# Reordering three weight and gate loads and six matmuls in the first microseconds of a gated attention/MLP kernel

## The chip, the cores and the metric

The kernel runs on one core of a Trainium2 chip. The metric is the device time of one execution in microseconds (us). The kernel before the change takes 206.35 us, the median of 4 runs (206.03 to 206.88).

## What is computed

One input `x` of 2048 rows by 512 goes through two branches, and a gate of one number per row mixes them:

```python
g = sigmoid((x * gate_w).sum(-1, keepdims=True))
# branch a: linear attention, 32 heads of 16, softmax feature maps of q and k
# branch b: gated MLP that mixes along the sequence
z  = gelu(x @ w_in)                    # 2048 x 1376
z1 = z[..., :688]
z2 = layernorm(z[..., 688:])
b  = (z1 * (w_sp @ z2 + b_sp)) @ w_out
out = g * a + (1 - g) * b
```

Only the very first part of branch b matters here: `x @ w_in[:, 688:]` for the first two tiles of 128 rows of `x`, and the dot product of these rows with `gate_w`.

## The kernel before, in words

The 2048 rows are 16 tiles of 128. For a matmul a tile of `x` must lie transposed in SBUF (`xT`), with the 512 inputs as four blocks `dt` of 128 partitions. Tiles 2 to 15 are transposed by DMA on the way in. Tiles 0 and 1 are loaded straight (`xs`, lines 119 and 120) and transposed by TensorE with an identity matrix (`x_T`, line 278).

The right half of `w_in` is held in `w_z2`, also in four blocks `dt`, each 128 partitions by 688 columns (172 KB), and each fetched by a DMA of its own (`load_z2w`, line 116). A tile's `z2` is a sum over the four blocks, in two halves `j` of 344 columns that lie in two PSUM banks: eight matmuls. The gate rides along: the four blocks of `gate_w`, loaded as four rows into `gaterow` (line 124), are turned by one small matmul (`gate_T`, line 288) and put as column 688 into `w_z2`, so that the second half is 345 columns wide and its last column is the gate's dot product.

`z2_first_two` (line 215) does this for tiles 0 and 1 together, in an order written out by hand, since the weights are still arriving. It begins with seven matmuls on constants into a buffer that is overwritten later (`warm_up`), then the transposes, then:

- `one(tt, dt, j)` is one of the matmuls of tile `tt`, block `dt`, half `j`.
- `z_part(tt, 0, 344, True)` is block 0's second half without the gate's column, since that column isn't there yet. `z_part(tt, 344, 345, False)` adds the missing column later.
- `gate_T()` may stand anywhere ahead of the first matmul that is 345 wide.

TensorE (PE) and ScalarE (ACT) run their instructions in the order of the program text; nothing rearranges them. DMAs are issued by SyncE (SP) and ScalarE, each with a queue of its own (in the profile, q1 is SP's queue and q10 is ScalarE's). Before the change the order of issue is

- SP: `x` tile 0, block 0, block 2, block 3, then the transposing loads of tiles 2 and 3, the left half of `w_in` (line 135), and all else that is loaded;
- ScalarE: `x` tile 1, block 1, gate row, then a table load and a small activation (line 127) that prepare the first gelu.

After `z2_first_two` come `z2` of tiles 2 and 3, `z1` of tiles 0 to 3, and so on for all tiles. The second, longer part of the kernel does the attention branch and the mixing along the sequence. Its matmuls are the largest groups of the profile, and the change touches none of them.

Of the kernel before, what the change touches and what calls it, by code (L numbers as in the profile page):

```python
# [14 lines left out]
P = 128  # L15
# [6 lines left out]
HF = FH // 2  # L22
NT = S // P
NDT = D // P
# [11 lines left out]
def kernel(  # L36
# [14 lines left out]
    nc = tc.nc  # L51
# [41 lines left out]
    gaterow = early.tile([P, P], BF16, name="gaterow")  # L93
# [11 lines left out]
        out=ramp[:, 0, :], data0=ones32[:, :], data1=zeros[:, :], initial=0.0,  # L105
# [4 lines left out]
    for q in range(4):  # L110
        qs = slice(32 * q, 32 * q + 32)
        nc.vector.tensor_tensor(
            out=ident[qs, qs], in0=ramp[qs, 0, :], in1=ramp[qs, 1, :], op=ALU.is_equal)
    nc.gpsimd.memset(brow[:], 0.0)
    nc.gpsimd.memset(wphi[:], 0.0)
    def load_z2w(eng, dt):
        eng.dma_start(out=w_z2[:, dt, 0:FH], in_=w_in_v[:, dt, FH:F])

    nc.sync.dma_start(out=xs[:, 0, :], in_=x2[0:P, :])  # L119
    nc.scalar.dma_start(out=xs[:, 1, :], in_=x2[P:2 * P, :])  # L120
    load_z2w(nc.sync, 0)
    load_z2w(nc.scalar, 1)
    load_z2w(nc.sync, 2)
    nc.scalar.dma_start(out=gaterow[0:NDT, :], in_=gate_w.rearrange("(dt p) -> dt p", p=P))
    load_z2w(nc.sync, 3)
    scrap = early.tile([P, 1], BF16, name="scrap")
    nc.scalar.activation(
        out=scrap[:, :], in_=nc.const_aps.tensor(1.0, [P, 1], BF16), func=AF.Gelu_apprx_tanh)
# [5 lines left out]
    for h in range(2):  # L134
        nc.sync.dma_start(
            out=w_z1[:, 2 * h:2 * h + 2, :], in_=w_in_v[:, 2 * h:2 * h + 2, 0:FH])
    for i in range(4, 8):
        x_dma_T(i)
    for q in range(2, NCH):
        nc.sync.dma_start_transpose(  # L140
            out=xT[:, :, q * CH:(q + 1) * CH], in_=x2[q * CH:(q + 1) * CH, :]
        )
    nc.sync.dma_start(out=brow[0:NT, :], in_=B_b_sp.rearrange("(t p) -> t p", p=P))
    for qk in (1, 0):
        nc.sync.dma_start_transpose(
            out=wqkT[:, qk * NDT:(qk + 1) * NDT, :], in_=A_wqkv[:, qk * D:(qk + 1) * D])
# [4 lines left out]
    for h in range(2):  # L151
        nc.sync.dma_start(
            out=wv_sb[:, 2 * h:2 * h + 2, :],
            in_=A_wqkv[h * 2 * P:(h + 1) * 2 * P, 2 * D:3 * D].rearrange("(dt p) n -> p dt n", p=P),
        )
    for q in range(NCH):
        nc.sync.dma_start_transpose(
            out=wspT[:, :, q * CH:(q + 1) * CH], in_=B_w_sp[q * CH:(q + 1) * CH, :]
# [4 lines left out]
        out=mask4[:], in_=mask4[:], pattern=[[-32, NG]],  # L163
# [3 lines left out]
        out=mask4[:], in_=mask4[:], pattern=[[32, NG]],  # L167
# [3 lines left out]
        out=mask64[:, :, :], in_=mask4[:, :, None].to_broadcast([P, NG, DH]))  # L171
# [7 lines left out]
    def next_turn(kind, n):  # L179
        turn[kind] += 1  # L180
        return f"{kind}{(turn[kind] - 1) % n}"

    def zp_tile():
        return psA.tile([P, 2, CH], FP32, name="zp", tag=next_turn("zp", 3))

    def pq_tile(shape, dtype=FP32):
        return psF.tile(shape, dtype, name="pq", tag=next_turn("pq", 2))

    def z_one(zp, tt, wt, w, dt, j, skip=False):
        n = HF if j == 0 else w - HF  # L190
        nc.tensor.matmul(  # L191
            zp[:, j, 0:n], lhsT=xT[:, dt, tt * P:(tt + 1) * P],
            rhs=wt[:, dt, j * HF:j * HF + n],
            start=(dt == 0), stop=(dt == NDT - 1), skip_group_check=skip,
        )
# [8 lines left out]
    def z2_out(tt, zp):  # L204
        z2v = z2all[:, tt, :].rearrange("p (j n) -> p j n", j=2)
        nc.scalar.activation(out=z2v, in_=zp[:, :, 0:HF], func=AF.Gelu_apprx_tanh)  # L206
        nc.vector.tensor_copy(out=glog[:, tt:tt + 1], in_=zp[:, 1, HF:HF + 1])
        for j in range(2):
            nc.vector.bn_stats(out=bn6[:, tt, j, :], in_=z2v[:, j, :])  # L209
        nc.vector.bn_aggr(out=mv[:, tt, :], in_=bn6[:, tt, :, :].rearrange("p j s -> p (j s)"))  # L210
# [4 lines left out]
    def z2_first_two():  # L215
        zps = [zp_tile() for _ in range(2)]
        tp1 = psA.tile([P, 2, P], BF16, name="tp1", tag=next_turn("zp", 3))
        turn["zp"] -= 1

        def warm_up(n, w=CH):  # L220
            for _ in range(n):
                nc.tensor.matmul(
                    zps[0][:, 1, 0:w], lhsT=nc.const_aps.tensor(1.0, [P, P], BF16),
                    rhs=nc.const_aps.tensor(1.0, [P, w], BF16), start=True, stop=True)

        def one(tt, dt, j):
            z_one(zps[tt], tt, w_z2, FH + 1, dt, j, skip=True)

        def z_part(tt, c0, c1, start):
            nc.tensor.matmul(  # L230
                zps[tt][:, 1, c0:c1], lhsT=xT[:, 0, tt * P:(tt + 1) * P],
                rhs=w_z2[:, 0, HF + c0:HF + c1], start=start, stop=False, skip_group_check=True)

        warm_up(6)
        warm_up(1, P)
        x_T(0, 0, 1, pq_tile([P, 1, P], BF16)[:, :, :])
        x_T(0, 1, NDT, pq_tile([P, 3, P], BF16)[:, :, :])
        x_T(1, 0, 2, tp1[:, :, :])
        x_T(1, 2, NDT, pq_tile([P, 2, P], BF16)[:, :, :], on_act=True)
        one(0, 0, 0)  # L240
        z_part(0, 0, HF, True)
        gate_T()
        one(0, 1, 0)
        one(1, 0, 0)
        z_part(1, 0, HF, True)
        one(1, 1, 0)
        for tt in range(2):
            one(tt, 1, 1)
        for tt in range(2):
            one(tt, 2, 0)  # L250
            one(tt, 2, 1)
            z_part(tt, HF, HF + 1, False)
        for tt in range(2):
            one(tt, 3, 0)
            one(tt, 3, 1)
            z2_out(tt, zps[tt])
# [21 lines left out]
    def x_T(i, d0, d1, tp, on_act=False):  # L278
        for dt in range(d0, d1):
            nc.tensor.transpose(tp[:, dt - d0, :], xs[:, i, dt * P:(dt + 1) * P], ident[:, :])  # L280
        dst = xT[:, d0:d1, i * P:(i + 1) * P]
        if on_act:
            nc.scalar.copy(out=dst, in_=tp)
        else:
            with tc.high_priority():
                nc.vector.tensor_copy(out=dst, in_=tp)

    def gate_T():
        gt = pq_tile([P, NDT])
        nc.tensor.matmul(gt[:, :], lhsT=gaterow[:, :], rhs=ident[:, 0:NDT], start=True, stop=True)  # L290
        nc.vector.tensor_copy(out=w_z2[:, :, FH], in_=gt[:, :])
# [27 lines left out]
    with tc.manual_schedule(engines={mybir.EngineType.PE, mybir.EngineType.Activation}):  # L319
        z2_first_two()  # L320
        z2_tile(2)
        z2_tile(3)
        for c in range(NCH):
            ts = list(range(c * 4, c * 4 + 4))
            for tt in ts:
                if c > 0:
                    z2_tile(tt)
                if c >= 2 and tt % 4 == 1:
                    later = fold(3 - c)
            for tt in ts:  # L330
                z1_tile(tt)
                if c >= 2 and tt % 2 == 0:
                    later.pop(0)()
            z2_norm(ts)
            if c == 1:
                b_T()
                turn["zp"] += 1
# [306 lines left out]
```

## Time and profile before

| | us |
|---|---|
| median of 4 runs | 206.35 |
| the profiled execution | 207.08 |
| its span (first to last instruction) | 205.3 |
| TensorE busy in the span | 201.1 (98%) |
| VectorE busy | 130.4 (63%) |
| ScalarE busy | 74.6 (36%) |
| first `z2` matmul begins | 5.07 |
| first gelu of `z2` begins (tile 0 done) | 8.00 |

Times within an execution are counted from the start of the span. PE is TensorE's matmuls, PEld its weight loads, DVE is VectorE, POOL is GpSimd. "SPq" and "ACTq" in front of an operation mean that the engine's sequencer issues a DMA; the number beside it is the time of the issue, not of the transfer. The ends of matmuls are modelled, so starts are the safer thing to read: the distance between two starts is what a matmul costs in a stream.

### The profile page before, as it was taken

What the parts mean: (1) busy time and instruction counts of PE and PEld (TensorE: products, weight loads), DVE (VectorE), ACT (ScalarE), POOL (GpSimd) and SP (SyncE); (2) the same over time, 40 slices, a digit from 0 to 9 for tenths busy, and PEclk for the clock granted to TensorE, in tenths of its full rate; (3) what the DMA queues carried; (4) which work ended last, traced back from release to release, by engine and by line L of the source; (5) the groups of instructions that cost most, each with busy time, mean ns of one, the idle gap of its engine ahead of it and who ended that gap; (6) DMA issues with size and microseconds to landing.
All of it is one profiled execution on the core that took longest, in us unless ns stands there. A gap on an engine that the chain in (4) does not pass through costs nothing.

```text
span 205.3 us, 3996 instructions
## 1 busy us (share of the span) xinstructions
PE 201.1 (98%) x1557; PEld 120.1 (59%) x1557; DVE 130.4 (63%) x283; ACT 74.6 (36%) x122; POOL 45.6 (22%) x76
## 2 busy tenths in 40 slices
PE   7999999999999999999999999999999999999994
PEld 3666666665666555556565666555555555665642
DVE  4377565746977677969797788555566645633332
ACT  3456677786222233333424032222251136002303
POOL 3020202020532326244242442222204220200000
DMA  6999499999998026940413228763566458452933
GB/s 197 255 207 189 92 243 210 249 191 267 189 251 180 3 38 148 315 84 14 91 30 63 51 38 110 142 117 74 103 165 80 90 107 188 58 96 54 155 65 104
DMA packets 89931, 27.22 MB, mean 133 GB/s; under 512 B 84184, under 2 KB 89912, under 8 KB 89912
## 3 DMA queue, kind: packets, MB, share of 16 engines
q1 hardware_dynamic: 87744, 24.99, 63.0%
q10 hardware_dynamic: 2168, 1.98, 3.6%
q8 instruction: 12, 0.20, 0.4%
q14 instruction: 7, 0.06, 0.1%
HBM read 4.15 MB, written 2.10 MB: 30 GB/s over the span
## 4 chain that ended last, share of the span: by engine, by line
PE 96%; DMA 2%; SPq 0%; DVE 0%; issue 0%
PE mm L454 36%; PE zp L191 18%; PE mm L355 14%; PE mm L515 8%; PE mm L509 7%; PE mm L395 7%; PE kvacc L411 2%; DMA w_z<-in_B_w_in_dram 2%; PE at L467 2%; PE mm L520 1%; PE zp L307 0%; PE at L478 0%; PE zp L230 0%; SPq L119 0%; PE pq L307 0%; DVE ob L527 0%
## 5 line engine op out<-in xcount | busy, mean ns | idle before, releaser
L454 PE MATMUL mm<-z2all,wspT 128*128 128x344 bf16 x512 | 79.9, 309 | 0.0
L454 PEld LDWEIGHTS <-wspT 128*128 128x128 bf16 x512 | 49.0, 98 | 25.3
L191 PE MATMUL zp<-w_z,xT 128*128 128x344 bf16 (+1 forms) x254 | 38.4, 311 | 0.6 <-DMA w_z<-in_B_w_in_dram 0.6
L359 ACT ACTIVATE eq<-mm 128x512 bf16<-128x512 f32 x32 | 17.4, 595 | 51.4 <-PE mm L355 25.7
L363 DVE TENSOR_REDUCE zs<-eq 128x64 f32<-128x1024 bf16 x16 | 19.5, 1220 | 20.1 <-ACT eq L359 20.1
L191 PEld LDWEIGHTS <-xT 128*128 128x128 bf16 x254 | 24.5, 98 | 12.0
L359 ACT ACTIVATE ek<-mm 128x512 bf16<-128x512 f32 x32 | 17.3, 601 | 27.1 <-PE mm L355 27.1
L459 DVE SCALAR_TENSOR_TENSOR ucat<-mm,bT,z1all 128x344 bf16<-128x344 f32 x32 | 17.4, 544 | 15.1 <-PE mm L454 15.1
L372 POOL TENSOR_TENSOR eq<-eq,ratio 128x512 bf16<-128x512 bf16 x16 | 16.9, 1056 | 44.6 <-DVE ratio L371 36.6
L531 ACT ACTIVATE ob<-mm,g_inv 128x512 bf16<-128x512 f32 (+1 forms) x15 | 10.1, 679 | 33.1 <-PE mm L520 28.5
L363 DVE TENSOR_REDUCE zs<-ek 128x64 f32<-128x1024 bf16 x16 | 19.2, 1208 | 2.8 <-ACT ek L359 2.8
L515 PE MATMUL mm<-wspT,uT 128*128 128x512 bf16 (+2 forms) x85 | 20.1, 367 | 0.0
L355 PEld LDWEIGHTS <-xT 128*128 128x128 bf16 x128 | 12.2, 98 | 12.0
L372 POOL TENSOR_TENSOR ek<-ek,ratio 128x512 bf16<-128x512 bf16 x16 | 16.9, 1056 | 2.2 <-DVE ratio L371 1.7
L509 PE MATMUL mm<-wspT,oT 128*128 128x512 bf16 (+2 forms) x68 | 16.6, 366 | 0.0
L355 PE MATMUL mm<-wq_p,xT 128*128 128x512 bf16 x64 | 16.4, 379 | 0.0
L395 PE MATMUL mm<-wv_sb,xT 128*128 128x512 bf16 x64 | 16.4, 379 | 0.0
L355 PE MATMUL mm<-wk_p,xT 128*128 128x512 bf16 x64 | 16.3, 379 | 0.0
L209 DVE BATCH_NORM_STATS2 bn<-z2all 128x6 f32<-128x344 bf16 x32 | 14.9, 502 | 0.0
L206 ACT ACTIVATE z2all<-zp 128x688 bf16<-128x688 f32 x16 | 11.8, 743 | 8.3 <-PE zp L191 8.2
L260 ACT ACTIVATE z1all<-zp 128x688 bf16<-128x688 f32 x16 | 11.9, 743 | 5.1 <-PE zp L191 4.7
L515 PEld LDWEIGHTS <-uT 128*128 128x128 bf16 x85 | 8.1, 98 | 9.4 <-issue 0.2
(77 smaller groups left out, 142.8 us busy)
## 6 DMA issues: line engine op xcount, KB each, us to landing
out_dram<-ob ACTq DMA_DIRECT2D x12, 128.0 KB, 2.5
wspT<-in_B_w_out_dram SPq DMA_DIRECT2D x2, 640.0 KB, 4.9
w_z<-in_B_w_in_dram SPq DMA_DIRECT2D x2, 344.0 KB, 4.6
w_z<-in_B_w_in_dram SPq DMA_DIRECT2D x3, 172.0 KB, 3.8
wv_sb<-in_A_wqkv_dram SPq DMA_DIRECT2D x2, 256.0 KB, 2.8
wspT<-in_A_wo_dram SPq DMA_DIRECT2D x2, 256.0 KB, 3.7
out_dram<-ob SPq DMA_DIRECT2D x3, 128.0 KB, 1.8
uT<-ucat SPq DMA_TRANSPOSE x16, 2.8
```

What stands on the lines that cost most here:

```text
L191: nc.tensor.matmul(zp[:, j, 0:n], lhsT=xT[:, dt, tt * P:(tt + 1) * P], rhs=wt[:, dt, j * HF:j * HF + n], start=(dt == 0), stop=(dt == NDT ...
L209: nc.vector.bn_stats(out=bn6[:, tt, j, :], in_=z2v[:, j, :])
L260: nc.scalar.activation(out=z1all[:, tt, :].rearrange("p (j n) -> p j n", j=2), in_=zp[:, :, 0:HF], func=AF.Gelu_apprx_tanh,)
L355: nc.tensor.matmul(ps[:, :], lhsT=xT[:, dt, tt * P:(tt + 1) * P], rhs=w[:, dt, :], start=(dt == 0), stop=(dt == NDT - 1))
L359: nc.scalar.activation(out=e[:, :, a, :], in_=ps[:, :].rearrange("p (h f) -> p h f", f=DH), func=AF.Exp, scale=1.0 - 2.0 * a)
L363: nc.vector.tensor_reduce(out=z[:].rearrange("p h a -> p (h a)"), in_=e[:].rearrange("p h a f -> p (h a) f"), axis=AX.X, op=ALU.add,)
L372: nc.gpsimd.tensor_tensor(out=e[:, :, 1, :], in0=e[:, :, 1, :], in1=ratio[:, :, None].to_broadcast([P, H, DH]), op=ALU.mult)
L395: nc.tensor.matmul(v_ps[:, :], lhsT=xT[:, dt, tt * P:(tt + 1) * P], rhs=wv_sb[:, dt, :], start=(dt == 0), stop=(dt == NDT - 1))
L454: nc.tensor.matmul(gp[:, 0:HF], lhsT=wspT[:, st, tt * P:(tt + 1) * P], rhs=z2all[:, st, j * HF:(j + 1) * HF], start=(st == 0), stop=(st == ...
L459: nc.vector.scalar_tensor_tensor(out=ucat[tt % NU][:, c0 + j * HF:c0 + (j + 1) * HF], in0=gp[:, 0:HF], scalar=bT[:, tt:tt + 1], in1=z1all[ ...
L509: nc.tensor.matmul(acc, lhsT=oTs[tt][:, g, :], rhs=wo_t[:, g, c0:c1], start=start and g == 0, stop=stop and g == NG - 1)
L515: nc.tensor.matmul(acc, lhsT=uTs[tt][:, i + ft, :], rhs=w_main[i][:, ft, c0:c1], start=start and ft == 0, stop=False)
```

## The change

Two orders change, and nothing else. On ScalarE the gate row is issued second and block 1 third, instead of the other way round. SP's DMAs keep their order. On TensorE the matmuls that need only block 0 come first for both tiles, with `gate_T` between the second tile's two, and block 1 is used afterwards.

```diff
     nc.sync.dma_start(out=xs[:, 0, :], in_=x2[0:P, :])
     nc.scalar.dma_start(out=xs[:, 1, :], in_=x2[P:2 * P, :])
     load_z2w(nc.sync, 0)
+    nc.scalar.dma_start(out=gaterow[0:NDT, :], in_=gate_w.rearrange("(dt p) -> dt p", p=P))
+    load_z2w(nc.sync, 2)
     load_z2w(nc.scalar, 1)
-    load_z2w(nc.sync, 2)
-    nc.scalar.dma_start(out=gaterow[0:NDT, :], in_=gate_w.rearrange("(dt p) -> dt p", p=P))
     load_z2w(nc.sync, 3)
...
         one(0, 0, 0)
         z_part(0, 0, HF, True)
+        one(1, 0, 0)
         gate_T()
+        z_part(1, 0, HF, True)
         one(0, 1, 0)
-        one(1, 0, 0)
-        z_part(1, 0, HF, True)
         one(1, 1, 0)
```

The order on TensorE, block by block, is then: before `0 0 | gate | 1 0 0 1`, after `0 0 0 | gate | 0 1 1` (the digits are the blocks `dt` that the matmuls of 344 columns read). From there on both kernels do the same: the second halves of block 1, then blocks 2 and 3.

Each DMA counts its landing on one of eight semaphores, given out in turn. With the swap the gate row takes the one that block 1 had, and block 1 the gate row's. SP's later issue of tile 4's transposing load (line 131) waits for the semaphore that block 1 had before, and so for the gate row after; that of tile 6 waits for block 1 instead of the gate row.

## The prediction

> **What bounds the kernel now.** I read the page first, its busy times and the chain that ended last:
>
> ```profile
> PE 201.1 (98%) x1557; PEld 120.1 (59%) x1557; DVE 130.4 (63%) x283; ACT 74.6 (36%) x122; POOL 45.6 (22%) x76
> ...
> PE 96%; DMA 2%; SPq 0%; DVE 0%; issue 0%
> ```
>
> TensorE is the bound, and 2% of the chain is a DMA. The list of what PE waited for says which:
>
> ```profile
> PE zp L222 <- PEq L628: 0.8, 1, 0.8
> PE zp L191 <- DMA w_z<-in_B_w_in_dram: 0.6, 1, 0.6
> ```
>
> These two are all of it. The same list for 8 us to the end is empty: once past the first two tiles PE waits for no other engine and no DMA. So whatever the start gains or loses by about 8 us is handed to the end one for one, and nothing else in the kernel can pay or charge. The chain of the first 9 us shows how the start hangs together:
>
> ```profile
> 1.25 3.78 DMA w_z<-in_B_w_in_dram
> 5.03 0.04 issue
> 5.07 0.45 PE zp L191
> ```
>
> Block 0 is issued at 1.25, has landed at 5.03, and the first z2 matmul starts at 5.07. The timeline shows what stands around it:
>
> ```profile
> 1.24 0.46 ACTq L117 DMA_DIRECT2D w_z<-in_B_w_in_dram  x1
> ...
> 1.74 0.57 ACTq L124 DMA_DIRECT2D gaterow<-in_gate_w_dram  x1
> ...
> 4.21 0.15 PEld L191 LDWEIGHTS <-xT 128*128 128x128 bf16 x1
> ...
> 5.07 0.45 PE L191 MATMUL zp<-w_z,xT 128*128 128x344 bf16 x1 [0.55 <-DMA w_z<-in_B_w_in_dram]
> ...
> 5.31 0.49 PE L230 MATMUL zp<-w_z,xT 128*128 128x344 bf16 x1
> ...
> 5.60 0.21 PE L290 MATMUL pq<-ident,gaterow 128*128 128x4 bf16 x1
> ...
> 5.67 0.74 PE L191 MATMUL zp<-w_z,xT 128*128 128x344 bf16 x2
> ...
> 6.20 0.39 PE L230 MATMUL zp<-w_z,xT 128*128 128x344 bf16 x1
> ...
> 6.43 0.90 PE L191 MATMUL zp<-w_z,xT 128*128 128x344 bf16 x5
> ```
>
> Three things are to be seen. PE had the first matmul's weights by 4.21 + 0.15 = 4.36, so the most that an earlier block 0 can give is 5.07 − 4.36 = **0.71 us** of start. From 5.07 to 6.43 five long matmuls and the gate's small one take 1.36 us; less 0.07 for the small one (5.60 to 5.67) that is **0.26 us** a long one. From 6.43 five take 0.73 us (to the 1-column matmul at 7.16), **0.146 us** each. So a matmul pulled ahead of 6.4 takes 0.26 there and saves only 0.146 later. And the gate matmul starts 0.29 us after the one ahead of it, about the slow pace; the late gate row costs PE nothing there.
>
> **The change, part by part.** *Block 0's landing.* The queues in 2.8 to 3.4 us, and then in 3.4 to 4.2 us (packets, MB, share of the DMA engines; q1 is SP's, q10 ScalarE's):
>
> ```profile
> q1 hardware_dynamic: 87, 0.11, 65.9%
> q10 hardware_dynamic: 56, 0.06, 42.2%
> ```
>
> ```profile
> q10 hardware_dynamic: 102, 0.11, 44.0%
> q1 hardware_dynamic: 92, 0.11, 48.2%
> ```
>
> The two queues share the engines about evenly, at 0.17 MB per 0.6 us and 0.22 MB per 0.8 us, some 0.28 MB/us. q10 here is nearly all block 1 (172 KB); it takes room that block 0 could have had. After the change ScalarE issues the gate row at 1.24 for 0.57 us and block 1 only then, at 1.81: a slip of 0.57 us, not an absence. Upper end: all of the 0.17 MB gets out of block 0's way, 0.17 / 0.28 = 0.61 us. Middle: only what q10 moved in the first 0.57 us of its run gets out of the way, 0.06 × 0.57 / 0.6 = 0.057 MB, 0.20 us. Lower end: nothing, if block 0's last packets are late for a reason of their own; all four blocks need 3.8 to 4.0 us from issue to landing, although they compete to different degrees. I take 0.3, nearer to the 0.20, since that follows from the slip itself: block 0 lands at 4.73, the first matmul starts at 4.77.
>
> *Block 1's landing.* It took 4.0 us from its issue. The slip alone puts it at 1.81 + 4.0 = 5.81. Ends: 1.81 + 3.8 = 5.61 (the quickest of line 117's DMAs) and 1.81 + 4.8 = 6.61 (the slowest of all into this tile, from line 135). After the change PE needs it behind four long matmuls and the gate, 1.36 − 0.26 = 1.10 us after its start: 4.77 + 1.10 = 5.87. It is there, with 0.06 us to spare. Without that cover each late tenth costs about a tenth.
>
> *Gate row.* It is issued 0.5 us earlier and no longer stands behind block 1's 172 KB; PEld's 0.3 us wait for it, hidden behind a running matmul, goes, gain 0. The copy of its column (DVE, line 291) is needed by the first matmul of 345 columns. From the gate matmul's start to that copy's end it is 5.60 to 6.05, 0.45 us. After the change three long matmuls stand between, 0.44 us at the quick pace, 0.78 at the slow: cost 0 to 0.02, I take 0.
>
> *SP.* Its DMAs keep their order. Tile 4's transposing load starts at 5.24, as block 1 lands, while SP was free at 4.04 + 1.08 = 5.12. It will wait for the gate row instead and start up to 0.12 us earlier; tile 6's, at 7.78, waits for block 1, long there. Nobody waits for either: 0, below as above. Tile 1's own transposed copy, needed one step earlier now, ends at 4.41 + 0.28 = 4.69, ahead of its use at 4.77 + 0.5.
>
> *The sum.* PE starts 0.3 us earlier and, with the pace changing at 6.43 as in this trace, does 0.3 / 0.26 = 1.15 more long matmuls by then; each saves 0.146 later: **0.17 us**. If the slow pace lasted to the end of these two tiles the whole 0.3 would stay. Against the profiled execution: span 205.3 − 0.17 = 205.1, and 207.08 − 0.17 = 206.9 with the 1.78 around the span. That execution lies 0.7 above the median; the median becomes 206.35 − 0.17 = **206.2 us**.
>
> [...] The granted clock reads 1.00 in both 5.07 to 6.43 and 6.43 to 8.00, yet the pace differs by 1.7. [...]
>
> [...]
>
> **The rivals.** *Nothing moves*: block 0's tail is its own. For it: equal landing times of all four blocks. Against it: the shares above. Time 206.35.
>
> *The whole start*: block 0 lands before 4.36, PE begins 0.71 us earlier. For it: the upper end of 0.61 us. Against it: block 1 slips by only 0.57 and then shares again. With the slow pace up to 6.4 it gives 0.71 / 0.26 × 0.146 = 0.40 us, 205.95; with the slow pace throughout 0.71, 205.64.
>
> *Block 1 becomes the wait*, the slower side. PE stands before its first block 1 matmul, with four long ones done. Break-even: before, PE starts its sixth long matmul at 6.43; after, that is 0.26 us behind the landing, so the loss begins when block 1 lands later than 6.43 − 0.26 = 6.17. At 6.61, before has 5 + 0.18 / 0.146 = 6.2 long matmuls done, after 4: 2.2 × 0.146 = 0.32 us lost, 206.7. If the quick pace were there from the start, before would end its 16 long matmuls at 5.07 + 16 × 0.146 = 7.41 (and the gate's small one besides, in both) and after the last 12 of them at 6.61 + 12 × 0.146 = 8.36: up to 0.95 lost, 207.3. For it: a spare of only 0.06 us, and one row at 4.8. Against it: the gate row is small, and by bytes all four blocks are there no later than now.
>
> **How the numbers follow.** Forecast (206.2, between 205.9 and 206.3): 0.45. Nothing moves: 0.15. The whole start, in its larger form: 0.20. Block 1 late: 0.20, of which 0.03 stays under the bound. A measurement of this kernel can tell about 0.3%, 0.62 us, from no change: faster needs 205.73 or less, slower 206.97 or more. So faster 0.20, same 0.45 + 0.15 + 0.03 = 0.63, slower 0.17. The range, 205.5 to 207.0, takes in the whole start and most of the late block 1; it leaves out the worst of the latter and of the scatter (the four runs span 0.85 us).
>
> **What would show it.** Right: the first z2 matmul at 4.7 to 4.9, no wait ahead of the first block 1 matmul, tile 0's gelu at 7.8 instead of 8.00, and the rest as it was. Wrong: a first matmul still at 5.0; or "PE zp waits for DMA w_z" listed twice, the second ahead of line 191's third matmul; or a change of pace that has moved away from 6.4, in which case the start says little about the total.

## The result

| | before | after |
|---|---|---|
| median, us (runs) | 206.31 (68) | 207.04 (44) |
| the profiled execution | 207.08 | 207.24 |
| its span | 205.3 | 205.5 |
| block 0 landed | 5.03 | 4.33 |
| first `z2` matmul begins | 5.07 | 4.37 |
| block 1 landed | 5.22 | 6.42 |
| first gelu of `z2` begins | 8.00 | 8.17 |

The ratio of the times is **1.0026**, with a 95% interval of 1.0015 to 1.0037: the change made the kernel slower, by about 0.54 us of 206.31 (206.31 × 0.0026); the two medians, over all runs, lie 0.73 us apart. The forecast was 0.17 us faster.

### The profile page after: what moved, and what is told of

The parts are those of the page before. It is cut to its first block, busy times and chain, and to the rows that moved or that the text cites. A ratio compares the mean times of both kernels' runs of the same rounds, so it can differ in the third digit from the quotient of the medians.

```text
span 205.5 us, 3997 instructions
## 1 busy us (share of the span) xinstructions
PE 201.0 (98%) x1557; PEld 120.0 (58%) x1557; DVE 130.4 (63%) x283; ACT 74.7 (36%) x122; POOL 45.8 (22%) x76
## 4 chain that ended last, share of the span: by engine, by line
PE 95%; DMA 2%; DVE 0%; ACTq 0%; issue 0%
PE mm L454 36%; PE zp L191 18%; PE mm L355 14%; PE mm L515 8%; PE mm L509 7%; PE mm L395 7%; DMA w_z<-in_B_w_in_dram 2%; PE kvacc L411 2%; PE at L467 2%; PE mm L520 1%; PE zp L307 0%; PE at L478 0%; PE pq L307 0%; DVE ob L527 0%; ACTq L122 0%; DVE ramp L108 0%
## 5 line engine op out<-in xcount | busy, mean ns | idle before, releaser
L531 ACT ACTIVATE ob<-mm,g_inv 128x512 bf16<-128x512 f32 (+1 forms) x15 | 10.1, 680 | 33.0 <-PE mm L520 28.5
```

## The profile after

On the page TensorE is still the bound, and a DMA's share of the chain is still 2%:

```profile
PE 201.0 (98%) x1557; PEld 120.0 (58%) x1557; DVE 130.4 (63%) x283; ACT 74.7 (36%) x122; POOL 45.8 (22%) x76
...
PE 95%; DMA 2%; DVE 0%; ACTq 0%; issue 0%
```

What TensorE waited for in the kernel after (us in total, times, longest):

```profile
PE zp L222 <- PEq L628: 0.8, 1, 0.8
PE zp L191 <- DMA w_z<-in_B_w_in_dram: 0.8, 1, 0.8
```

The second line has the same words as before, and 0.8 in the place of 0.6. But it is another block. The chain of its first 9.5 us says which:

```profile
1.58 0.26 ACTq L122
1.84 0.03 issue
1.87 4.56 DMA w_z<-in_B_w_in_dram
6.42 0.04 issue
6.46 1.04 PE zp L191 x6
```

Before, the chain began with the DMA issued at 1.25, block 0. Now it begins with the issue of the gate row on ScalarE (line 122), and behind it at 1.87 stands block 1, which needs 4.56 us. The timeline of the kernel after shows the same on TensorE:

```profile
1.25 0.59 ACTq L122 DMA_DIRECT2D gaterow<-in_gate_w_dram  x1
...
4.37 0.45 PE L191 MATMUL zp<-w_z,xT 128*128 128x344 bf16 x1
...
5.25 0.38 PE L230 MATMUL zp<-w_z,xT 128*128 128x344 bf16 x1
...
6.46 1.04 PE L191 MATMUL zp<-w_z,xT 128*128 128x344 bf16 x6 [0.84 <-DMA w_z<-in_B_w_in_dram]
```

The wait for block 0 is gone, the four matmuls of block 0 begin at 4.37 instead of 5.07, and the next matmul in the program's order has to wait for block 1: 0.84 us of idle time, in brackets on the last line. Blocks 2 and 3 are later as well, 6.23 and 6.74 where they had landed at 5.59 and 6.02, and so are the transposed tiles 2 and 3, 7.79 and not 7.07. Past 8.2 us TensorE waits for nothing, as before. The gelu is 0.17 later (8.00 to 8.17), and the span 0.2.

The view of the DMAs in 3.4 to 5.0 us became the key to the rest. Before, and then after:

```profile
DMA packets 534, 0.51 MB, mean 319 GB/s; under 512 B 188, under 2 KB 534, under 8 KB 534
```

```profile
DMA packets 352, 0.38 MB, mean 235 GB/s; under 512 B 89, under 2 KB 352, under 8 KB 352
```

Loads are outstanding in both during these 1.6 us, and after the change a quarter fewer bytes arrive (0.38 for 0.51 MB). A slip of one issue by 0.6 us doesn't by itself say why.

## The experiments

Theory **L** says that block 1 lands too late and TensorE stands before it; its rival **R**, that the new order of matmuls costs by itself. Later ones ask why block 1 is so late: **S**, the loads as a whole slacken, whichever block comes second; **G**, the early gate row does it; **T**, the transposing load behind; **Q**, two queues must have weights to move from the start; **P**, something about block 1; **A**, a block that flows alone reads a narrow stretch of memory. "Landed" gives blocks 0, 1, 2, 3 in us from the start of the span; MB are those of 3.4 to 5.0 us. Landings, waits and views are those of one profiled execution of each kernel; times are medians, and ratios are against runs of the kernel before on the same chip. The edits are shown against the kernel after, with `...` for what is left out.

**1. pe_only**: the new order on TensorE with the old order of DMAs.

```diff
-    nc.scalar.dma_start(out=gaterow[0:NDT, :], in_=gate_w.rearrange("(dt p) -> dt p", p=P))
-    load_z2w(nc.sync, 2)
     load_z2w(nc.scalar, 1)
+    load_z2w(nc.sync, 2)
+    nc.scalar.dma_start(out=gaterow[0:NDT, :], in_=gate_w.rearrange("(dt p) -> dt p", p=P))
```

> The new order on TensorE, with the DMA order of before (block 1 second on ScalarE, gate row third). Theory L (block 1 is late because ScalarE issues it 0.6 us later): block 0 lands near 5.0 and block 1 near 5.2 as before, TensorE starts near 5.1 and waits no second time; time within 0.1% of before. Rival R (the new order of matmuls costs something by itself, such as the gate's column coming late): slower than before by about the 0.26% of the change.

Measured: 206.36, ratio 0.9992 (0.9977 to 1.0008). Landed 4.50, 4.76, 5.20, 5.67; gelu at 7.76; TensorE waits for no DMA. Its flow is that of before or better:

```profile
DMA packets 529, 0.59 MB, mean 367 GB/s; under 512 B 113, under 2 KB 529, under 8 KB 529
```

R falls: its 0.26% lies outside the interval, and the order of matmuls costs nothing that can be measured here.

**2. dma_only**: the new order of DMAs with the old order on TensorE.

```diff
         one(0, 0, 0)
         z_part(0, 0, HF, True)
-        one(1, 0, 0)
         gate_T()
-        z_part(1, 0, HF, True)
         one(0, 1, 0)
+        one(1, 0, 0)
+        z_part(1, 0, HF, True)
```

> The new DMA order (gate row second, block 1 third on ScalarE), with the old order on TensorE, which needs block 1 after only two long matmuls. Theory L: TensorE starts near 4.4, does two long matmuls and the gate, and stands until block 1 lands near 6.4; against the changed kernel two more matmuls of 0.146 us are still to do by then, so slower than before by 0.26% + 0.14% = 0.4%. Rival R (the order of matmuls is what costs): within 0.1% of before, or faster.

Measured: 207.55, ratio 1.0061 (1.0036 to 1.0085). Landed 4.01, 6.46, 6.24, 6.76. The timeline of its profiled execution:

```profile
4.36 0.49 PE L191 MATMUL zp<-w_z,xT 128*128 128x344 bf16 x1
4.64 0.49 PE L230 MATMUL zp<-w_z,xT 128*128 128x344 bf16 x1
...
6.50 0.73 PE L191 MATMUL zp<-w_z,xT 128*128 128x344 bf16 x2 [1.36 <-DMA w_z<-in_B_w_in_dram]
...
9.42 1.26 PE L191 MATMUL zp<-w_z,xT 128*128 128x344 bf16 x5
```

Two long matmuls are done when block 1 becomes the wait, not four, and 1.36 us are lost before it. With pe_only this puts the whole loss on the side of the DMAs, and the new order of matmuls hides a part of it. This execution (209.35; 3 of the 12 are above 209) also kept the slow pace to 10.2 us: the last line's five matmuls take 1.26 us, about 0.25 each, at 9.4 us. That is taken up again below.

**3. one_queue**: block 1 on SP's queue, between blocks 0 and 2; ScalarE keeps `x` tile 1 and the gate row.

```diff
     nc.scalar.dma_start(out=gaterow[0:NDT, :], in_=gate_w.rearrange("(dt p) -> dt p", p=P))
+    load_z2w(nc.sync, 1)
     load_z2w(nc.sync, 2)
-    load_z2w(nc.scalar, 1)
```

> The changed kernel, but block 1 is issued by SP right behind block 0 and ahead of block 2, so that ScalarE issues only x tile 1 and the gate row. Theory L: block 0 lands near 4.3, block 1 near 5.3, before TensorE needs it near 5.5; no second wait; the early start is kept, 0.3 to 0.4 us faster than before (0.15% to 0.2%). Rival S (the four blocks' last packets come late whatever the order, and the early block 0 only moves the waiting to block 1): block 1 lands near 6 and TensorE stands again; 0 to 0.3% slower than before.

Measured: 207.68, ratio 1.0052 (1.0036 to 1.0069). Landed 3.93, 5.52, 6.09, 6.55; 0.31 MB. Tile 0's gelu begins at 7.27, 0.7 earlier than in the profile of before, and yet the span is 205.9. What TensorE waited for:

```profile
PE zp L222 <- PEq L628: 0.8, 1, 0.8
PE pq L307 <- DVE mv L210: 0.6, 1, 0.6
PE zp L191 <- DMA w_z<-in_B_w_in_dram: 0.5, 1, 0.5
```

Block 1 at 5.52 lies between L's 5.3 and S's 6, and TensorE does wait a second time, for 0.5 us. The middle line is new, at 26.5 us. SP has one issue more (0.45 to 0.5 us), so all that it issues later slips: tiles 2 and 3 land at 7.59, and the attention branch begins with a wait. In one_queue_gate_late (5), which has the same issues on SP, this wait is put down to `wphi`, small loads of SP's. SP is 0.5 us behind at 10.9 us and 2.7 at 26.2 (line 152 at 26.17 for 23.51); why the lag grows stays open. An early gain is given back later, and this kernel doesn't serve as a better version.

**4. b2_on_act**: after, with blocks 1 and 2 exchanged between the queues (SP 0, 1, 3; ScalarE gate row, then 2).

```diff
-    load_z2w(nc.sync, 2)
-    load_z2w(nc.scalar, 1)
+    load_z2w(nc.sync, 1)
+    load_z2w(nc.scalar, 2)
```

> The changed kernel with blocks 1 and 2 exchanged: SP issues blocks 0, 1, 3 and ScalarE issues block 2 third, behind the gate row. Theory L: block 2 takes over the late landing, near 6.2 to 6.4, where TensorE needs it only near 6.5; block 1 lands by 5.6; time 0.1% to 0.2% faster than before. Rival S: block 1 is late all the same (after 6), and the time is 0 to 0.3% above before.

Measured: 206.93, ratio 1.0022 (1.001 to 1.0035). Landed 3.92, 6.29, 6.71, 6.91; 0.33 MB; TensorE waits 1.1 us for block 1. So block 1 isn't late for standing on ScalarE's queue behind the gate row. It is late on SP's too, where it was next in line. L's simple form, in which only the block that is issued late lands late, falls here; S stands.

**5. one_queue_gate_late**: one_queue, with the clearing of `gaterow` on VectorE moved behind two other preparations, so that the gate row's issue would be late.

```diff
-    nc.vector.memset(gaterow[:], 0.0)
...
+    nc.vector.memset(gaterow[:], 0.0)
...
+    load_z2w(nc.sync, 1)
     load_z2w(nc.sync, 2)
-    load_z2w(nc.scalar, 1)
```

> As one_queue (SP issues blocks 0, 1, 2, 3; new order on TensorE), but the gate row is issued by ScalarE only after its table load, near 2.8 us, so that no 256-byte rows are under way while block 0 flows. Theory G (the gate row sent ahead of the weights is what slackens the DMAs from 3.4 us on): the flow stays at 0.14 MB per 0.4 us as with the old DMA order, block 3 lands near 6.0 instead of 6.55, time at or below before. Theory Q (one block alone in flight is what slackens them): 0.05 to 0.10 MB per 0.4 us between 3.4 and 4.6 again, block 3 near 6.5, time 0.3% to 0.5% above before.

Measured: 207.57, ratio 1.0053 (1.004 to 1.0067). Landed 3.94, 5.41, 5.91, 6.35; 0.29 MB. The edit didn't delay what it was to delay: the gate row was still issued at 1.36, and the run says only that one_queue repeats. It shows besides that ScalarE's order need not be that of the text, which was said ahead of the prediction: the table load of line 127, which the text has behind the gate row, starts at 1.24 here, ahead of the gate row's issue.

**6. slip_gate_third**: block 1 is second on ScalarE and the gate row third, but block 1 is held back to 1.79, where it stands after the change, by a copy of one column into its buffer. ScalarE's first instructions are kept in the order of the text.

```diff
+    nc.vector.tensor_copy(out=w_z2[:, 1, 0:1], in_=ramp[:, 1, 0:1])
...
     load_z2w(nc.sync, 0)
-    nc.scalar.dma_start(out=gaterow[0:NDT, :], in_=gate_w.rearrange("(dt p) -> dt p", p=P))
-    load_z2w(nc.sync, 2)
     load_z2w(nc.scalar, 1)
+    load_z2w(nc.sync, 2)
+    nc.scalar.dma_start(out=gaterow[0:NDT, :], in_=gate_w.rearrange("(dt p) -> dt p", p=P))
```

> New order on TensorE; on ScalarE block 1 is issued second as before, but held back to near 1.8 us by a one-column copy of VectorE into its buffer, and the gate row is issued third. So block 1 slips as in the change, without a gate row ahead of it. Theory G: no slackening, block 1 lands near 5.3 to 5.6, time at or below before. Theory Q: slackening as in the change, block 1 near 6.3, time about 0.2% to 0.3% above before.

Measured: 207.53, ratio 1.0043 (1.0028 to 1.0059). Landed 4.09, 6.07, 6.27, 6.65, the gate row at 6.22, which is what TensorE waited for here (0.8 us). Its flow in 3.4 to 5.0 us:

```profile
DMA packets 266, 0.31 MB, mean 194 GB/s; under 512 B 43, under 2 KB 266, under 8 KB 266
```

The flow slackens with no gate row ahead, so the early gate row isn't needed for it: G falls.

**7. gate_pool**: the reverse. Block 1 is second on ScalarE, at 1.25 beside block 0, and the gate row goes early, at 1.42, on GpSimd's queue.

```diff
-    nc.scalar.dma_start(out=gaterow[0:NDT, :], in_=gate_w.rearrange("(dt p) -> dt p", p=P))
-    load_z2w(nc.sync, 2)
     load_z2w(nc.scalar, 1)
+    nc.gpsimd.dma_start(out=gaterow[0:NDT, :], in_=gate_w.rearrange("(dt p) -> dt p", p=P))
+    load_z2w(nc.sync, 2)
```

> New order on TensorE; on ScalarE block 1 is issued second at 1.24 us as before; the gate row is issued early by GpSimd on a queue of its own. Blocks 0 and 1 are in flight together. Theory G: the early gate row slackens the DMAs here too, block 3 lands near 6.6, time up to 0.3% above before. Theory Q: no slackening, block 0 near 4.5 to 5.0, block 1 near 5.0, block 3 near 5.7 to 6.0, time within 0.1% of before.

Measured: 206.6, ratio 1.0008 (0.9998 to 1.0019). Landed 4.27, 4.57, 5.02, 5.53; gelu at 7.15.

```profile
DMA packets 674, 0.57 MB, mean 355 GB/s; under 512 B 302, under 2 KB 674, under 8 KB 674
```

An early gate row does the flow no harm either. With 6 this leaves, for these edits, the place of block 1's issue: beside block 0's, or 0.6 us behind.

**8. late_transposes**: after, with the transposing load of tiles 2 and 3 (`x_dma_T(2, 2)`) moved behind the two loads of line 135.

```diff
-    x_dma_T(2, 2)
...
+    x_dma_T(2, 2)
```

> The changed kernel, with the transposing load of x tiles 2 and 3 issued behind the two loads of the left half of w_in instead of ahead of them. Theory T (the transposing load's 256-byte packets, queued behind block 3, are what delays the last packets of blocks 1 and 2): block 1 lands before 5.8. Theories G and Q: block 1 lands after 6 as in the change. The transposed tiles come later, so the time itself may rise.

Measured, one run: 209.21. Landed 4.03, 6.70, 6.33, 7.34; 0.32 MB. TensorE waits 1.4 us for block 1 and 1.5 for the tiles moved, which come at 10.17. Block 1 is no earlier without the transposing load beside it: T falls.

**9. split_pair**: blocks 0 and 1 each as two halves of 64 rows, one on each queue; blocks 2 and 3 in one DMA; the gate row on GpSimd. Here and in 10 to 12 ScalarE's first instructions are kept in the order of the text, as in 6.

```diff
...
+        load_z2w(nc.sync, 0, slice(0, 64))
+        load_z2w(nc.scalar, 0, slice(64, P))
+        load_z2w(nc.sync, 1, slice(0, 64))
+        load_z2w(nc.scalar, 1, slice(64, P))
+        nc.gpsimd.dma_start(out=gaterow[0:NDT, :], in_=gate_w.rearrange("(dt p) -> dt p", p=P))
+        nc.sync.dma_start(out=w_z2[:, 2:4, 0:FH], in_=w_in_v[:, 2:4, FH:F])
```

> New order on TensorE; blocks 0 and 1 are each fetched as two halves of 64 rows, one half by SP and one by ScalarE, in the order block 0, block 1 on both; blocks 2 and 3 come as one DMA of SP; the gate row is issued by GpSimd. So the two queues work side by side from the start, and block 0 is still first. Theory Q (the DMAs slacken when one block flows alone ahead of the others): no slackening, 0.12 to 0.15 MB per 0.4 us from 2.6 to 4.6, block 0 lands near 4.0, block 1 near 4.6, blocks 2 and 3 by 6; TensorE starts near 4.4 without a second wait for block 1; 0.1% to 0.3% faster than before. Rival P (block 1's place in time, not the company it flows in, is what is slow): slackening after 3.4, block 1 near 5.5, no gain.

Measured: 207.37, ratio 1.0063 (1.0035 to 1.009). Block 0's halves landed at 4.06 (ScalarE) and 5.15 (SP), block 1's at 5.34 and 5.56, the rest at 7.06; 4 of 12 runs were at 208.92 to 209.18, the profiled one among them, which keeps the slow pace to 10.1.

```profile
DMA packets 308, 0.34 MB, mean 210 GB/s; under 512 B 64, under 2 KB 308, under 8 KB 308
```

Both queues have weights to move from the start, but of the same block, and the flow is slack. Q, in its words, falls.

**10. b2_pair**: block 2 beside block 0 on ScalarE, block 1 behind block 0 on SP, the gate row third on ScalarE.

```diff
...
         load_z2w(nc.sync, 0)
-    nc.scalar.dma_start(out=gaterow[0:NDT, :], in_=gate_w.rearrange("(dt p) -> dt p", p=P))
-    load_z2w(nc.sync, 2)
-    load_z2w(nc.scalar, 1)
+        load_z2w(nc.scalar, 2)
+        load_z2w(nc.sync, 1)
+        nc.scalar.dma_start(out=gaterow[0:NDT, :], in_=gate_w.rearrange("(dt p) -> dt p", p=P))
```

> New order on TensorE; ScalarE issues block 2 second, at 1.24, beside block 0, and the gate row third; SP issues blocks 0, 1, 3. Two blocks flow side by side from the start, but the second is block 2. Theory Q: no slackening (0.12 to 0.15 MB per 0.4 us between 3.4 and 4.6), block 0 near 4.8, block 1 near 5.3, block 3 near 6; time within 0.15% of before. Rival P (block 1 is slow whenever it doesn't flow together with block 0): slackening as in the change, block 1 near 6.2, time 0.2% or more above before.

Measured: 206.64, ratio 1.0001 (0.9988 to 1.0014). Landed 4.50, 5.08, 4.69, 5.56.

```profile
DMA packets 514, 0.56 MB, mean 351 GB/s; under 512 B 116, under 2 KB 514, under 8 KB 514
```

The flow is full with block 2 as the partner: P falls. Block 1 lands at 5.08 here, issued as late as in 4 and from the same queue, where it landed at 6.29. What differs, besides the gate row that 6 and 7 have cleared, is whether another whole block was issued beside block 0.

**11. b0_slips** and **12. b0_slips_again**: the two blocks' roles exchanged. SP issues the gate row second and block 0 third, at 1.68; ScalarE block 1 second, at 1.25.

```diff
...
+        nc.sync.dma_start(out=gaterow[0:NDT, :], in_=gate_w.rearrange("(dt p) -> dt p", p=P))
         load_z2w(nc.sync, 0)
-    nc.scalar.dma_start(out=gaterow[0:NDT, :], in_=gate_w.rearrange("(dt p) -> dt p", p=P))
-    load_z2w(nc.sync, 2)
-    load_z2w(nc.scalar, 1)
+        load_z2w(nc.scalar, 1)
+        load_z2w(nc.sync, 2)
```

> The slip turned round: SP issues the gate row second and block 0 third (near 1.85), ScalarE issues block 1 second at 1.24. Theory Q: now block 1 flows alone first, and the DMAs slacken after it in the same way, 0.05 to 0.10 MB per 0.4 us between 3.4 and 4.6, block 3 lands near 6.6. Rival P: no slackening. TensorE's start is later in any case.

> A second look at the slip turned round (SP: gate row second, block 0 third; ScalarE: block 1 second). Theory Q: slackening between 3.4 and 4.6 and block 3 near 6.6. If it again lies in between (0.10 to 0.13 MB per 0.4 us, block 3 near 6.2), the slackening grows with the time for which one block is alone: the slip is 0.43 us here, 0.62 in the change.

Measured: 206.79, and the second time 208.53. The first landed at 5.36, 5.18, 5.73, 6.18 with 0.47 MB; the second at 5.32, 4.08, 5.76, 6.20 with 0.34 MB. A slip of 0.43 us gives one execution between the two kinds of flow and one that is slack. Inconclusive: that the loss grows with the slip is suggested by it, not shown.

**13. after_again** and **14. before_again**: the two kernels unchanged, one more profiled execution each.

> The changed kernel once more, for a second look at the same landings. If the late block 1 belongs to the change: block 0 near 4.0 to 4.4, block 1 after 6.0, TensorE waits twice or, if block 0 is there before 4.36, once. If the first profile was an accident: block 1 near 5.5 and no wait for it.

> The kernel before once more. If two blocks side by side keep the flow: 0.10 to 0.15 MB per 0.4 us from 2.6 to 5.0, blocks 0 and 1 landed by 5.3, block 3 by 6.1.

Measured: after 207.15, landed 4.05, 6.33, 5.85, 6.57, wait 0.6 for block 1; 0.31 MB. Before 206.47, landed 4.34, 4.59, 5.09, 5.57; 0.56 MB. The flows repeat. The timeline of this second execution of before:

```profile
4.44 0.49 PE L191 MATMUL zp<-w_z,xT 128*128 128x344 bf16 x1
...
5.79 0.90 PE L191 MATMUL zp<-w_z,xT 128*128 128x344 bf16 x5
...
7.36 0.74 ACT L206 ACTIVATE z2all<-zp 128x688 bf16<-128x688 f32 x1 [2.30 <-PE zp L191]
```

and of the second at after:

```profile
6.37 1.04 PE L191 MATMUL zp<-w_z,xT 128*128 128x344 bf16 x6 [0.60 <-DMA w_z<-in_B_w_in_dram]
...
8.08 0.74 ACT L206 ACTIVATE z2all<-zp 128x688 bf16<-128x688 f32 x1 [3.07 <-PE zp L191]
```

Before begins at 4.44 here, with no wait for block 0, and its pace has changed by 5.8; the gelu starts at 7.36, not at 8.00. After's gelu stands where it stood, at 8.08 against 8.17.

**15. after_rows** and **16. one_queue_rows**: after and one_queue, with the rows of `w_in` dealt to the four blocks in turn, so that a block reads rows from the whole matrix and not 128 neighbouring ones. In these two kernels `z2` is therefore computed from permuted weights.

```diff
+    w_in_i = B_w_in.rearrange("(p dt) f -> p dt f", dt=NDT)
...
-        eng.dma_start(out=w_z2[:, dt, 0:FH], in_=w_in_v[:, dt, FH:F])
+        eng.dma_start(out=w_z2[:, dt, 0:FH], in_=w_in_i[:, dt, FH:F])
```

> The changed kernel, with the rows of w_in dealt out to the four z2 blocks in turn (row 4p+dt to partition p of block dt) instead of 128 neighbouring rows each; the values of z2 are then those of permuted inputs, the work and the bytes are the same. Theory A (the flow falls because all engines read one narrow stretch of memory together): no slackening, 0.12 to 0.15 MB per 0.4 us from 2.6 to 5.0, block 1 lands near 5.3 to 5.6, the early start is kept, 0.1% to 0.3% faster than before. Rival B (it has nothing to do with the addresses): slackening as in the change, block 1 after 6.0, 0.2% to 0.3% slower than before.

> one_queue (SP issues all four blocks in order) with the same dealing out of rows. Theory A: no slackening, block 1 near 4.8, block 3 near 5.9. Rival B: slackening, block 1 after 5.4, block 3 near 6.5.

Measured: after_rows 207.56, ratio 1.0074 (1.0043 to 1.0106), landed 4.48, 6.41, 6.19, 6.65, 0.40 MB; one_queue_rows 206.88 in one run, landed 3.94, 5.78, 6.22, 6.65, 0.32 MB. Both as slack as with neighbouring rows: A falls.

**All profiled executions together**, by the MB that arrived in 3.4 to 5.0 us:

| two whole blocks issued side by side at 1.24 to 1.27 | MB | one block issued alone ahead | MB |
|---|---|---|---|
| before, before_again | 0.51, 0.56 | after, after_again | 0.38, 0.31 |
| pe_only | 0.59 | dma_only | 0.33 |
| gate_pool | 0.57 | slip_gate_third, b2_on_act | 0.31, 0.33 |
| b2_pair | 0.56 | one_queue, one_queue_gate_late, one_queue_rows | 0.31, 0.29, 0.32 |
| | | late_transposes, split_pair | 0.32, 0.34 |
| | | after_rows | 0.40 |

The two groups don't overlap, and b0_slips (0.47, 0.34) lies between them and in the second. This is what was shown. The gate row, the transposing load, block 1's contents, the number of queues and the neighbouring rows have each been tried and don't account for it. No run separates whether it is the second block that matters or only the bytes issued by 1.27 us (344 KB for 172).

The traces tell a little more. In the slack executions packets still take 79 to 90% of the DMA engines' time, so a lack of work explains a part at most. The queues of one_queue in 3.4 to 5.0 us, and then of pe_only (packets, MB, share of the 16 engines' time; packets overlap, so a sum can pass 100%):

```profile
q1 hardware_dynamic: 254, 0.31, 87.4%
```

```profile
q1 hardware_dynamic: 386, 0.42, 76.8%
q10 hardware_dynamic: 143, 0.16, 28.9%
```

A byte took 1.6 times as long in one_queue (87.4 / 0.31 against 105.7 / 0.59). The median packet of 1376 B takes 59 ns in every execution; the difference is in a few that hang. Over 200 ns are 7 to 22 of them in the right-hand column, the longest 0.86 to 1.36 us, and 0 to 5 in the left-hand one, the longest 0.17 to 0.43. But in four of the five executions on the left 10 to 20 such packets come later, in 5.8 to 7.0 us, when the four blocks have landed and the loads of line 135 arrive; in the first profile of before there are 8 in 2.6 to 3.4, while block 0 is under way. So it isn't shown that the order of issue makes packets hang; it may only shift when they do. Why they hang stays open.

## Why the prediction was wrong, point by point

- **The failed step is block 1's landing.** It was costed as a slip alone, 1.81 + 4.0 = 5.81, with 0.06 us to spare. It came at 6.42 and 6.33. Of the 0.61 us in the first profile 0.06 is a later issue (1.87), the rest a longer way, 4.56 us from the issue instead of 4.0. The step took over a landing time from an execution in which blocks 0 and 1 were issued together, and the change ended just that. Its upper end, 6.61, held; the break-even of 6.17 was passed in both executions.
- **"By bytes all four blocks are there no later than now"** was too kind. Blocks 2 and 3 land 0.64 and 0.72 us later as well (6.23 for 5.59, 6.74 for 6.02), and only block 0 gained. (That the two queues share "about evenly" holds for 3.4 to 4.2 us, 44.0% and 48.2%; in 2.8 to 3.4 it was 42.2% and 65.9%, and 11 of q10's 56 packets there were still `x` tile 1.) From two queues (pe_only) block 1 landed at 4.76 with 0.59 MB, behind block 0 on one queue (one_queue) at 5.52 with 0.31 MB, 0.76 us later for an issue of 0.45 to 0.5. The number of queues isn't the reason, since after has two and is slack.
- **Block 0's landing** was taken at 4.73; it came at 4.33 and 4.05, earlier than the upper end of the gain, 5.03 − 0.61 = 4.42. TensorE got nearly the whole 0.71 us (4.37 for 5.07) that a rival spoke of, and then stood for 0.84 us ahead of block 1's matmuls.
- **The wait for block 0 itself**, on which the gain was built, belonged to one execution. In the four others with two blocks side by side (before_again, pe_only, gate_pool, b2_pair) block 0 is there by 4.27 to 4.50 and TensorE doesn't wait for it: there is hardly a gain to be had. The prediction had the clue, an execution 0.7 us above the median, and carried its 0.17 us over to the median all the same. In before_again, 0.61 us faster (206.47 for 207.08), the gelu begins 0.64 us earlier (7.36 for 8.00).
- **The rival "block 1 becomes the wait" came true**, and for this pair of profiles its price held. By its sum, at 6.46 before has 5 + 0.03 / 0.146 = 5.2 long matmuls done and after 4: 1.2 × 0.146 = 0.18 us lost; measured 0.17 in the gelu (8.17 for 8.00) and 0.16 in the profiled time. The start is handed to the end one for one, as the first step had it. The 0.54 us of the ratio is more than this price, since the usual execution of before is faster than the profiled one.
- **The moment at which the pace changes** was taken as fixed at 6.43, and no run shows a fixed moment: it lies at 6.4 in the profile of before, 5.8 in before_again, before 4.8 in gate_pool, 6.5 in pe_only; in one_queue the first two long matmuls start at 4.16 and 4.31, at the quick pace already. With an early start and an early change before is through tile 0 at 7.36, while after is held by a DMA, to 8.08. So two pairs of executions give 0.17 (8.17 for 8.00) and 0.72 (8.08 for 7.36) in the gelu, 0.16 (207.24 for 207.08) and 0.68 (207.15 for 206.47) in the time, and the 0.54 of the ratio lies between. The prediction knew this case as "up to 0.95 lost". It put 0.17 of this rival's 0.20 beyond its bound of 0.62 us, though its price at the pace as profiled was 0.32 at most; the two don't fit together. The executions here spread from 4.2 or earlier to 6.5 us, and in three of them (below) to 9.1 and beyond; what sets the moment was not shown.
- **Right**: the order of matmuls and the copies of tile 1 cost nothing (pe_only at 0.9992), TensorE doesn't wait for the gate row in the profile after, and past 8.2 us it waits for nothing.

No version beat the kernel before: pe_only 0.9992, b2_pair 1.0001 and gate_pool 1.0008 are equal to before within their intervals, though gate_pool's profile has the earliest gelu of all, 7.15.

## What to carry to other kernels

When a load is moved back so that another flows first, don't cost the moved one as its old latency plus the slip: that latency was measured beside its neighbours, and the spare has to stand the longest landing that the trace shows, not the usual one. Take more than one profile before building on a stall: the wait for block 0 stood in one of the five executions with two blocks side by side. Look at the load that is moved back as hard as at the one that is moved up, and take the profiled moment of a change of pace as one draw of several. A line in a list of waits that reads as before may belong to another load: check by its start.

## What the runs showed of the hardware

- One 172 KB load issued alone, with the next 0.4 to 0.6 us behind, lands early itself (3.92 to 4.48 us, split_pair's halves aside; 4.27 to 5.03 with two side by side) but is followed by a slack flow, 182 to 249 GB/s in 3.4 to 5.0 us, where two different blocks issued side by side are followed by 319 to 367 GB/s. Block 3, issued last, lands at 6.35 to 7.34 us, where it landed at 5.53 to 6.02. In the slack flow single packets hang, up to 1.36 us, against a median of 59 ns.
- In three profiled executions the slow pace lasted to 9.1 to 10.2 us: dma_only, split_pair and b0_slips_again. In dma_only TensorE had stood for 1.36 us in the middle of its first matmuls, in the other two it began at 5.2 to 5.4. Their times are 208.5 to 209.4. In dma_only 3 of 12 runs are above 209 and the others at 207.2 to 207.8, in split_pair 4 of 12 are above 208.9 and the others at 206.7 to 207.6; of before 2 of 68 are above 208.5, of after 2 of 44. That idle time early on keeps the pace slow fits these three and wasn't tested by itself. It isn't enough: b0_slips began at 5.40, as late as the others, and was quick from its first long matmul (starts at 5.40, 5.55, 5.69). In late_transposes the pace was quick from 4.3 us on, and a wait of 1.4 us behind that didn't bring the slow one back.
- The granted clock reads 1.00 in these three executions, and 0.998 to 1.000 over all the profiled ones, though the distance between long matmuls is 0.25 to 0.29 us before the change of pace and 0.146 behind it.
- With one more issue of 0.45 to 0.5 us on SP in the first 3 us, a wait of 0.6 us stood at 26.5 us in one_queue and one of 0.7 in one_queue_gate_late, and none in one_queue_rows; in one_queue SP's issues, 0.5 us behind at 10.9 us, were 2.7 behind at 26.2.
